# Attention and two MLP layers on one core: the first token block kept on chip, Pool's work cut into pieces of 128 columns, second banks for h and y

## The chip, the cores and the metric

The kernel runs on one core of a Trainium2 chip. The metric is device time in microseconds (us), the median of several executions. Engines are named as in the profile: PE (matrix products), DVE (vector engine), ACT (scalar engine), POOL (GpSimd), SP (issues DMAs).

## The reference

```python
# q, k, v: (4, 8, 576, 64); x: (2304, 512); float32 values, 2304 = 4 * 576
scores = scale * q @ k.T
thresh = max(scores, -1) - tau                       # tau = 0.02
scores = where(scores >= thresh, scores, -1e9)
attn = exp(scores - max(scores, -1))
attn = attn / (sum(attn, -1) + 1e-9)
x = (attn @ v).transpose(0, 2, 1, 3).reshape(2304, 512)
h = x @ w_in                                         # 512 x 2048
x = (h / (1 + exp(-h))) @ w_out                      # 2048 x 512
x = ((x @ w_a) * (x @ w_b)) @ w_out2                 # 512 x 1536, 1536 x 512
```

The weights arrive as 64-bit floating point; the kernel sees each number as two 32-bit words.

## The kernel before

**Stages.** Attention is cut into 144 softmax tiles of 128 query rows by 576 keys. `softmax` makes one: `scores` (PE), `lowest` (DVE: negated scores and their minimum), `threshold` (DVE, one column, L497), `exp` (ACT), `mask` (DVE, L506, with the row sums as a by-product). The first 16 tiles are "early": they alternate between two PSUM banks (`sa`, `sb`) and read the scores from PSUM; the later ones read a copy in SBUF. `weigh` collects the tiles of half a head pair (4 tiles for 256 query rows, 5 for 320): PE turns the masked tiles, multiplies with v into bank `av`, ACT copies the result out (`evacuate`). The inverse row sums are turned by PE too, stored to DRAM (`r_d`), loaded back spread over 64 partitions each (`xi`), Pool multiplies (`divide`, L618), and x goes to DRAM (`xT_d`).

MLP1 runs over 9 blocks of 256 tokens and 16 slices f of the hidden size, 144 units. `load_x` loads a block of x (four quarters, `xr`) and splits it into a high part (ACT) and the rest (Pool, `xl`, L676). A unit is `mlp1_up`, 12 products of 256 columns into bank `hb` (L699), tanh on ACT, `gate` on DVE (L711, reads `hb` and releases it), a split of g on ACT and DVE (L717), and `mlp1_down`, 12 products (L746) that add up in `sb` over the 16 units of a block. After a block, ACT and DVE empty `sb` (L765). Up of unit n stands ahead of down of unit n-1. There is one `hb` and one `sb`; the early tiles use `sb` for scores as well.

MLP2 has 60 units (blocks of 512 tokens, 12 slices): 12 products into `ps_a`, 12 into `ps_b` (L825), ACT copies `ps_a`, DVE multiplies by `ps_b` (`z`, L835), the split into `zh` (ACT) and `zl` (DVE, L841), then 12 products into the outputs `op` (L869).

**Weights.** They pass `split_weight` in chunks of 128 x 512: 32 for MLP1, all of which a block of MLP1 needs, and 36 for MLP2, where the first four have room of their own and the others wait until block 8 of MLP1 has let go of MLP1's weights. The steps of a chunk: DMA into `wraw`, `low` (ACT), `scale` (ACT for MLP1, L317; DVE for MLP2, L319), `sign` (DVE, L323), `join` (DVE, L328), `total` (POOL, the sum of the two words, L332), `hi` (ACT, L336), `lo` (L340: Pool for MLP1, alternately Pool and DVE for MLP2). The scaled half `wc` has one buffer, which `total` releases; `wraw` and `wt` have two.

**Order.** No engine's order is written by hand. A planner (`Plan`) holds every step as a task with an engine, a cost, a rank, the tasks it needs, and rings of buffers it takes and releases. `run` plays through time: an engine that is idle takes the ready task with the lowest rank, and that order is emitted. So a cost or a ring that is altered can move instructions on every engine. Attention's ranks are the tile numbers (0 to 143), the weights of MLP1 spread from 2 in steps of 1.3, MLP1 lies from 1000, MLP2 from 1e5, and MLP2's weights from 1e6: PE takes work of MLP1 only where attention has none ready.

The planner has a rule for DVE and Pool, which it takes to share a way to memory:

```python
if t["port"]:
    shared = max(0, min(port["Pool" if e == "DVE" else "DVE"] - now, t["cost"]))
    port[e] = end = done = end + self.SHARED * shared
```

A task lengthens by the time for which the other engine's current one still runs.

## Time and profile before

| | |
|---|---|
| median of three runs | 1202.97 us (1200.87 to 1204.55) |
| the profiled execution | 1202.49 us, its span 1200.7 us |
| busy: PE, DVE, ACT, POOL | 97%, 54%, 45%, 23% |
| moved by DMA | 90.14 MB |
| chain that ended last | PE 76%, DVE 10%, DMA 5%, issue 4%, ACT 4%, POOL 1% |

All views are of one execution. A line number (L506) is one of the kernel above; "z<-ps_b,z" is what is written and what is read, by the program's names; "128x512" is partitions by elements. In a group, "x36 | 36.4, 1011 | 5.3 <-ACT e L503 5.0" reads: 36 instructions, 36.4 us in all, 1011 ns each; the engine was idle for 5.3 us just ahead of them, 5.0 of it ended by ACT's line 503. In a timeline the first number is the start in us, the second the duration, and the bracket the idle time ahead with what ended it. PEclk is the clock granted to PE, 1.00 being 2.4 GHz.

### The profile page before, as it was taken

To read this page: it belongs to the slowest core of one execution; us is meant where nothing else is said; L and a number is where in the kernel's file an instruction comes from. 1 tells how busy PE (TensorE), PEld (TensorE's weight loads), DVE (VectorE), ACT (ScalarE), POOL (GpSimd) and SP (SyncE) were. 2 spreads that over 40 slices of the span, in tenths; PEclk is the share of its full clock that TensorE was granted. 3 is DMA by queue.
4 is the path that set the end of the run, shared out by engine and by line. 5 is a ranking of instruction groups with operands and counts; after the bars stand their busy time and mean duration, and the time that the engine had idled before them with its cause. 6 is when DMAs were issued, how large, how long until landed. Compare 5 with 4: busy or idle time off the path is not lost.

```text
span 1200.7 us, 19670 instructions
## 1 busy us (share of the span) xinstructions
PE 1162.6 (97%) x7675; PEld 998.2 (83%) x7675; DVE 648.1 (54%) x1428; ACT 544.5 (45%) x1071; POOL 278.9 (23%) x232
## 2 busy tenths in 40 slices
PE   8889989999999999989999999999999999999998
PEld 5556667888888888889999999888888888888898
DVE  7989898777777777473233258765311211221121
...
GB/s 190 195 176 150 160 152 129 80 85 86 97 72 71 89 89 32 101 166 36 1 37 27 1 66 117 152 123 71 70 1 1 70 1 1 18 36 1 1 36 18
DMA packets 43276, 90.14 MB, mean 75 GB/s; under 512 B 4384, under 2 KB 22448, under 8 KB 43184
## 3 DMA queue, kind: packets, MB, share of 16 engines
...
q10 hardware_dynamic: 144, 0.00, 0.0%
...
## 4 chain that ended last, share of the span: by engine, by line
PE 76%; DVE 10%; DMA 5%; issue 4%; ACT 4%; POOL 1%; SPq 0%; DVEq 0%; ACTq 0%; POOLq 0%
PE op L869 12%; PE ps_b L825 12%; PE ps_a L825 12%; PE hb L699 12%; PE sb L746 12%; PE av L583 5%; PE tp L538 5%; PE sa L473 4%; DVE e L506 3%; DMA xi<-r_d 2%; DVE t L489 1%; DVE wraw L323 1%; DVE thr L497 1%; DVE wc L328 1%; DVE gl L717 1%
## 5 line engine op out<-in xcount | busy, mean ns | idle before, releaser
L699 PE MATMUL hb<-xh,w 128*128 128x256 f32 x1152 | 225.1, 290 | 6.0 <-DVE th L711 3.9
L699 PEld LDWEIGHTS hb<-xh,w 128*128 128x128 f32 x1152 | 179.3, 192 | 14.2 <-DVE th L711 6.2
L746 PE MATMUL sb<-gh,w 128*128 128x256 f32 x1152 | 169.6, 286 | 2.3 <-DVE yo L765 1.8
L699 PE MATMUL hb<-xl,w 128*128 128x256 f32 x576 | 162.9, 283 | 0.0
L835 DVE TENSOR_TENSOR z<-ps_b,z 128x512 f32<-128x512 f32 (+1 forms) x60 | 38.2, 636 | 230.2 <-PE ps_b L825 230.2
L746 PEld LDWEIGHTS sb<-gh,w 128*128 128x128 f32 x1152 | 150.5, 192 | 6.6 <-DVE yo L765 2.8
L506 DVE SCALAR_TENSOR_TENSOR e<-t,thr,e 128x576 f32<-128x576 f32 x128 | 129.7, 1014 | 21.8 <-ACT e L503 20.8
L825 PE MATMUL ps_a<-yh,w 128*128 128x512 f32 (+1 forms) x480 | 137.0, 370 | 0.0
L825 PE MATMUL ps_b<-yh,w 128*128 128x512 f32 (+1 forms) x480 | 136.6, 369 | 0.0
L869 PE MATMUL op<-w,zh 128*128 128x512 f32 x432 | 134.3, 392 | 0.0
L489 DVE TENSOR_SCALAR_CACHE_REDUCE t<-sa,nscale 128x576 f32<-128x576 f32 x128 | 103.6, 809 | 51.6 <-PE sa L473 49.6
L538 PE MATMUL tp<-ident,e 128*128 128x128 f32 x706 | 106.5, 280 | 13.9 <-DVE e L506 10.0
L711 DVE SCALAR_TENSOR_TENSOR th<-th,hb 128x256 f32<-128x256 f32 x144 | 60.2, 418 | 107.2 <-ACT th L708 106.8
L332 POOL TENSOR_TENSOR wt<-wc,wt 128x512 uint32<-128x512 uint32 x68 | 91.2, 1342 | 109.5 <-DVE wc L328 91.3
L503 ACT ACTIVATE e<-t,min 128x576 f32<-128x576 f32 x128 | 99.6, 780 | 28.2 <-DVE t L489 27.5
L708 ACT ACTIVATE th<-hb 128x256 f32<-128x256 f32 x144 | 55.0, 382 | 122.3 <-PE hb L699 113.2
L699 PEld LDWEIGHTS hb<-xl,w 128*128 128x128 f32 x576 | 110.1, 191 | 0.0
L538 PEld LDWEIGHTS tp<-ident,e 128*128 128x128 f32 x706 | 78.8, 141 | 37.4 <-DVE e L506 16.7
L832 ACT COPY z<-ps_a 128x512 f32<-128x512 f32 (+1 forms) x60 | 32.5, 542 | 162.5 <-PE ps_a L825 162.4
L825 PEld LDWEIGHTS ps_a<-yh,w 128*128 128x128 f32 x480 | 87.5, 188 | 16.7
L825 PEld LDWEIGHTS ps_b<-yh,w 128*128 128x128 f32 x480 | 86.8, 188 | 15.4
L717 DVE TENSOR_TENSOR gl<-th,gh 128x256 fp32r<-128x256 f32 x144 | 76.0, 528 | 36.8 <-ACT gh L714 36.4
...
## 6 DMA issues: line engine op xcount, KB each, us to landing
...
```

The source lines that it names most:

```text
L332: nc.gpsimd.tensor_tensor(out=s["t"], in0=s["c"].bitcast(U32), in1=s["t"], op=ALU.add)
L489: nc.vector.tensor_scalar(out=s["t"], in0=s["s"][:, :, :NH], scalar1=nscale, scalar2=None, op0=ALU.mult, op1=ALU.min, accum_out=s["min"])
L503: nc.scalar.activation(out=s["e"], in_=s["t"], func=AF.Exp, scale=-1.0, bias=s["min"])
L506: nc.vector.scalar_tensor_tensor(out=s["e"], in0=s["s"][:, :, :NH] if early else s["t"], scalar=s["thr"], in1=s["e"], op0=ALU.is_ge if ear ...
L538: nc.tensor.transpose(t["tp"][:, j * P:(j + 1) * P], e["e"][:, o:o + P], ident)
L583: nc.tensor.matmul(s["av"][h * D:(h + 1) * D, :nq], lhsT=v["v"][:, h, k], rhs=s["p"][:, k, h * nq:(h + 1) * nq], start=(k == 0), stop=(k = ...
L699: nc.tensor.matmul(s["h"], lhsT=w[:, a, o:o + P], rhs=xx, start=(c == 0 and k == 0), stop=(c == NC - 1 and k == 2))
L711: nc.vector.scalar_tensor_tensor(out=s["t"], in0=s["t"], scalar=1.0, in1=s["h"], op0=ALU.add, op1=ALU.mult)
L717: nc.vector.tensor_sub(out=s["gl"], in0=s["t"], in1=s["gh"].bitcast(F32))
L746: nc.tensor.matmul(ys[j][:, e, :], lhsT=w[:, a, e * P:(e + 1) * P], rhs=gs[j, f][g], start=(f == 0 and e % 2 == 0 and a == 1), stop=(f == ...
L825: nc.tensor.matmul(s[nm][:, :tn], lhsT=w[:, a, o:o + P], rhs=yy[:, :tn], start=(c == 0 and k == 0), stop=(c == NC - 1 and k == 2))
L869: nc.tensor.matmul(o_ps[t0, i], lhsT=s[z][:, i * P:(i + 1) * P], rhs=wt["o2", f][:, a, :], start=(f == 0 and k == 0), stop=(f == NF2 - 1 a ...
```

## The change

1. *x of block 0.* The first 256 query rows of the first batch are block 0 of MLP1. For them (`stays`) the inverse sums are written 64 times side by side by a wide reciprocal, four small products by the identity spread them over the partitions of bank `av`, ACT copies x and the inverses in one piece of 512 columns, Pool divides, and `split_x` (what `load_x` did inline) splits from there. The 16 DMAs of these four weighings go.
2. *Pieces.* Pool's `total`, `lo` of weights and of q, `divide` and `xl` are issued as instructions of 128 columns (107 to 115 where the size doesn't divide). The planner's rule for the port changes: DVE now waits only to the end of the current piece. Pool's planned cost gets 90 ns for each piece.
3. *Columns.* `guard` and `threshold` take their added constant from a column of SBUF.
4. *k's low part* (20 head splits from tile 54 on) moves from Pool to DVE.
5. *Second banks.* From unit 64 on, odd units of MLP1 use bank `hc` instead of `hb`; from block 4 on, even blocks use `sd` instead of `sb`. Both live in a pool that opens when attention has closed. The two banks of MLP2's `ps_a` and `ps_b` become two pools: one opens with attention's end, the other after MLP1.

```diff
+TWO_H = 64
+PIECE = 128
...
-                        shared = max(0, min(port["Pool" if e == "DVE" else "DVE"] - now, t["cost"]))
-                        port[e] = end = done = end + self.SHARED * shared
+                        other, piece = port["Pool" if e == "DVE" else "DVE"]
+                        end = done = end + (max(0, other - now) % piece if e == "DVE" else max(0, other - now))
+                        port[e] = end, pool_ns(PIECE)
...
 def pool_ns(n):
-    return int(2.35 * n + 90)
+    return int(2.35 * n + 90 * len(pieces(n)))
+
+def pieces(n):
+    k = -(-n // PIECE)
+    return [slice(n * i // k, n * (i + 1) // k) for i in range(k)]
...
         def total():
-            nc.gpsimd.tensor_tensor(out=s["t"], in0=s["c"].bitcast(U32), in1=s["t"], op=ALU.add)
+            for o in pieces(512):
+                nc.gpsimd.tensor_tensor(out=s["t"][:, o], in0=s["c"][:, o].bitcast(U32), in1=s["t"][:, o], op=ALU.add)
...
-            eng = nc.gpsimd if lo_engine == "Pool" else nc.vector
+            eng, parts = (nc.gpsimd, pieces(512)) if lo_engine == "Pool" else (nc.vector, [slice(0, 512)])
...
         def lo_k():
-            nc.gpsimd.tensor_tensor(...)
+            nc.vector.tensor_tensor(...)
...
-        q, k = (add("Pool", pool_ns(S), n + R_SPLIT, f, [up]) for f in (lo_q, lo_k))
+        q = add("Pool", pool_ns(S), n + R_SPLIT, lo_q, [up])
+        k = add("DVE", dve_ns(S), n + R_SPLIT, lo_k, [up], port=True)
...
         def guard():
-            ... scalar1=EPS, scalar2=None, op0=ALU.add)
+            ... scalar1=eps, scalar2=None, op0=ALU.add)
...
+            if wide:
+                s["wide"] = x_p.tile([P, 320], F32, name="xi")[:, :m * D].rearrange("p (m d) -> p m d", d=D)
+                nc.vector.reciprocal(out=s["wide"], in_=s["sum"][:, :m].rearrange("p (m o) -> p m o", o=1).broadcast_to((P, m, D)))
...
-                nc.vector.tensor_add(out=s["thr"], in0=s["min"], in1=tadd)
+                nc.vector.tensor_scalar(out=s["thr"], in0=s["min"], scalar1=tadd, scalar2=None, op0=ALU.add)
...
+        stays = b == 0 and half == 0
...
+            if stays:
+                for k in range(4):
+                    nc.tensor.matmul(s["av"][k // 2 * D:(k // 2 + 1) * D, nq + k % 2 * P:][:, :P], lhsT=inv["wide"][:, k, :], rhs=ident,
+                                     start=True, stop=True, skip_group_check=True)
...
+        if stays:
+            dv = add("Pool", pool_ns(nq), last_n + R_EV, divide, [ev])
+            att_tasks.append(split_x(0, c, lambda: s["x"], [dv], "x")[1])
+            return es
...
+        bank = "hc" if n >= TWO_H and n % 2 else "hb"
...
+        ring = "sd" if j * NF >= TWO_H and j % 2 == 0 else "sb"
...
-        pools["ab"] = pool(ctx, "ps_ab", 2, "right", space=PSUM)
+        pools["hc"] = pool(p1, "ps_hc", 1, space=PSUM)
+        pools["ab", 0] = pool(ctx, "ps_ab", 1, "right", space=PSUM)
...
+        pools["ab", 1] = pool(ctx, "ps_ab2", 1, space=PSUM)
```

Costs, rings and the port rule together give a new order. Ahead of tile 52 there are 14 units of MLP1 on PE now, where there were 16. Three places:

POOL, in the first chunks of weights (`L332`/`L344` is the sum, `L340`/`L353` the low part, `L618`/`L649` the division of x by its sums, `L676`/`L705` the rest of x; "x4" is four instructions in a row). Before:

```order
L332 TENSOR_TENSOR wt<-wc,wt 128x512
L340 TENSOR_TENSOR w<-wt,w 128x512
L332 TENSOR_TENSOR wt<-wc,wt 128x512
L618 TENSOR_TENSOR x<-x,xi 128x256
L340 TENSOR_TENSOR w<-wt,w 128x512
L332 TENSOR_TENSOR wt<-wc,wt 128x512
L340 TENSOR_TENSOR w<-wt,w 128x512
L676 TENSOR_TENSOR xl<-xr,xh 128x256
```

And now:

```order
L649 TENSOR_TENSOR x<-x 128x128 x2
L344 TENSOR_TENSOR wt<-wc,wt 128x128 x4
L705 TENSOR_TENSOR xl<-x,xh 128x128 x2
L353 TENSOR_TENSOR w<-wt,w 128x128 x4
L344 TENSOR_TENSOR wt<-wc,wt 128x128 x4
L353 TENSOR_TENSOR w<-wt,w 128x128 x4
L344 TENSOR_TENSOR wt<-wc,wt 128x128 x4
L649 TENSOR_TENSOR x<-x 128x128 x2
L353 TENSOR_TENSOR w<-wt,w 128x128 x4
```

Each sum and each low part is four instructions; x is divided and split between them without a load ahead of it.

DVE, in MLP2, from the product of unit 7 on (`L319`/`L330` scale, `L323`/`L334` sign, `L328`/`L339` join, `L340`/`L353` the low part of every second chunk). Before:

```order
L835 TENSOR_TENSOR z<-ps_b,z 128x512
L841 TENSOR_TENSOR zl<-z,zh 128x512
L319 TENSOR_SCALAR wc<-wraw 128x512
L340 TENSOR_TENSOR w<-wt,w 128x512
L323 TENSOR_SCALAR wraw<-wraw 128x512
L328 SCALAR_TENSOR_TENSOR wc<-wc,wraw 128x512
L319 TENSOR_SCALAR wc<-wraw 128x512
L323 TENSOR_SCALAR wraw<-wraw 128x512
L328 SCALAR_TENSOR_TENSOR wc<-wc,wraw 128x512
L835 TENSOR_TENSOR z<-ps_b,z 128x512
```

And now:

```order
L883 TENSOR_TENSOR z<-ps_b,z 128x512
L889 TENSOR_TENSOR zl<-z,zh 128x512
L330 TENSOR_SCALAR wc<-wraw 128x512
L353 TENSOR_TENSOR w<-wt,w 128x512
L334 TENSOR_SCALAR wraw<-wraw 128x512
L339 SCALAR_TENSOR_TENSOR wc<-wc,wraw 128x512
L330 TENSOR_SCALAR wc<-wraw 128x512
L334 TENSOR_SCALAR wraw<-wraw 128x512
L339 SCALAR_TENSOR_TENSOR wc<-wc,wraw 128x512
L330 TENSOR_SCALAR wc<-wraw 128x512
L334 TENSOR_SCALAR wraw<-wraw 128x512
L353 TENSOR_TENSOR w<-wt,w 128x512
```

Three chunks begin where two did between one product and the next: DVE is given MLP2's weights in a closer order.

PE, in MLP2 at unit 8 (`L825`/`L873` are the products into `ps_a` and `ps_b`, `L869`/`L917` the ones into the outputs; the last chunk of this unit is the 32nd of MLP2's). Before:

```order
L825 MATMUL ps_a<-yl,w 128x512
L825 MATMUL ps_a<-yh,w 128x512 x2
L825 MATMUL ps_a<-yl,w 128x512
L825 MATMUL ps_b<-yh,w 128x512 x2
L825 MATMUL ps_b<-yl,w 128x512
L825 MATMUL ps_b<-yh,w 128x512 x2
L825 MATMUL ps_b<-yl,w 128x512
L825 MATMUL ps_b<-yh,w 128x512 x2
L825 MATMUL ps_b<-yl,w 128x512
L825 MATMUL ps_b<-yh,w 128x512 x2
L825 MATMUL ps_b<-yl,w 128x512
L869 MATMUL op_9786<-w,zh 128x512 x2
```

And now:

```order
L873 MATMUL ps_a<-yl,w 128x512
L917 MATMUL op_10199<-w,zh 128x512 x2
L917 MATMUL op_10199<-w,zl 128x512
L917 MATMUL op_10204<-w,zh 128x512 x2
L917 MATMUL op_10204<-w,zl 128x512
L917 MATMUL op_10211<-w,zh 128x512 x2
L917 MATMUL op_10211<-w,zl 128x512
L917 MATMUL op_10221<-w,zh 128x512 x2
L917 MATMUL op_10221<-w,zl 128x512
L873 MATMUL ps_a<-yh,w 128x512 x2
L873 MATMUL ps_a<-yl,w 128x512
L873 MATMUL ps_b<-yh,w 128x512 x2
```

The twelve products of unit 7 into the outputs, which followed all of unit 8's, now stand between those into `ps_a`, and `ps_b` comes after them. Between the seventh and the 32nd chunk of MLP2 lie 25 chunks, in the old order and in the new.

## Rows read from the trace of the kernel before

**Rows 1.** The page, part 1: busy us, share of the span, instructions.

```profile
PE 1162.6 (97%) x7675; PEld 998.2 (83%) x7675; DVE 648.1 (54%) x1428; ACT 544.5 (45%) x1071; POOL 278.9 (23%) x232
```

**Rows 2.** Busy time by stretch; columns: stretch, each engine's busy us, PEclk, DMA, GB/s.

```profile
0.00:57.00 57.00, 47.32 (x323) 31.30 (x323) 48.14 (x122) 44.33 (x78) 27.60 (x29) 1.00 0.59 194
57.00:190.00 133.00, 121.27 (x860) 86.90 (x860) 122.29 (x265) 101.24 (x202) 77.14 (x60) 0.97 0.49 153
190.00:490.00 300.00, 293.57 (x2350) 259.75 (x2350) 225.32 (x594) 197.52 (x379) 88.41 (x72) 1.00 0.25 82
490.00:545.00 55.00, 50.42 (x397) 48.41 (x394) 32.81 (x62) 23.54 (x54) 15.00 (x13) 0.97 0.44 141
...
705.00:752.00 47.00, 45.24 (x353) 43.17 (x352) 36.28 (x64) 24.98 (x52) 21.72 (x16) 1.00 0.36 113
```

**Rows 3.** Groups of instructions by form, 57 to 190 us, DVE and PE.

```profile
L506 DVE SCALAR_TENSOR_TENSOR e<-t,thr,e 128x576 f32<-128x576 f32 x36 | 36.4, 1011 | 5.3 <-ACT e L503 5.0
...
L323 DVE TENSOR_SCALAR wraw<-wraw 128x512 uint32<-128x512 uint32 x23 | 20.9, 909 | 3.0 <-ACT wc L317 3.0
...
L497 DVE TENSOR_TENSOR thr<-min,tadd 128x1 f32<-128x1 f32 x35 | 13.6, 390 | 0.3
...
L699 PE MATMUL hb<-xh,w 128*128 128x256 f32 x124 | 26.5, 305 | 1.5 <-POOL w L340 1.5
```

**Rows 4.** Groups by form, whole span: the mask of an early tile.

```profile
L506 DVE SCALAR_TENSOR_TENSOR e<-sa,thr,e 128x576 f32<-128x576 f32 x8 | 6.5, 814 | 1.2 <-ACT e L501 1.2
```

**Rows 5.** Timeline of POOL, then of DVE, MLP2's weights (start us, us, instruction).

```profile
765.84 1.29 POOL L332 TENSOR_TENSOR wt<-wc,wt 128x512 uint32<-128x512 uint32 x1 [1.10 <-DVE wc L328]
...
769.40 1.30 POOL L332 TENSOR_TENSOR wt<-wc,wt 128x512 uint32<-128x512 uint32 x1 [2.27 <-DVE wc L328]
...
771.42 1.35 POOL L340 TENSOR_TENSOR w<-wt,w 128x512 fp32r<-128x512 f32 x1 [0.73 <-ACT w L336]
...
773.41 1.67 POOL L332 TENSOR_TENSOR wt<-wc,wt 128x512 uint32<-128x512 uint32 x1 [0.63 <-DVE wc L328]
...
767.62 0.43 DVE L323 TENSOR_SCALAR wraw<-wraw 128x512 uint32<-128x512 uint32 x1
...
771.65 1.68 DVE L328 SCALAR_TENSOR_TENSOR wc<-wc,wraw 128x512 uint32<-128x512 uint32 x1
```

**Rows 6.** Timeline of PE around attention's end.

```profile
499.68 0.40 PE L699 MATMUL hb<-xh,w 128*128 128x256 f32 x2
...
502.56 0.40 PE L699 MATMUL hb<-xh,w 128*128 128x256 f32 x2
...
507.05 0.50 PE L699 MATMUL hb<-xh,w 128*128 128x256 f32 x2 [1.46 <-DVE th L711]
...
513.39 1.96 PE L746 MATMUL sb<-gh,w 128*128 128x256 f32 x8 [1.76 <-DVE yo L765]
...
526.40 0.50 PE L699 MATMUL hb<-xh,w 128*128 128x256 f32 x2 [1.18 <-DVE th L711]
```

**Rows 7.** Timeline of POOL at 29 and 50 us, then of DVE at 50 us.

```profile
29.35 0.73 POOL L618 TENSOR_TENSOR x<-x,xi 128x256 f32<-128x256 f32 x1 [1.09 <-DMA xi<-r_d]
...
50.13 1.29 POOL L340 TENSOR_TENSOR w<-wt,w 128x512 fp32r<-128x512 f32 x1 [0.96 <-ACT w L336]
...
51.38 0.92 POOL L676 TENSOR_TENSOR xl<-xr,xh 128x256 fp32r<-128x256 f32 x1
...
50.72 0.08 DVE L506 DVE_READ_ACCUMULATOR e<-sb,thr,e 128x1 f32 x1
```

**Rows 8.** Timeline of PE, first and last of ten units of MLP1's last stretch.

```profile
715.81 0.40 PE L699 MATMUL hb<-xh,w 128*128 128x256 f32 x2
...
744.37 0.41 PE L699 MATMUL hb<-xh,w 128*128 128x256 f32 x2
```

**Rows 9.** Timeline of DVE, then of PE: the 32nd chunk of MLP2's weights.

```profile
816.01 0.69 DVE L340 TENSOR_TENSOR w<-wt,w 128x512 fp32r<-128x512 f32 x1
...
817.58 0.62 PE L825 MATMUL ps_b<-yh,w 128*128 128x512 f32 x2
```

More of the change, by code (lines that the diff above doesn't have):

```diff
@@ L125, in run @@
         pipe, window, cold, spans = 0, 0, False, [(0, 4400)]
-        port = {"DVE": 0, "Pool": 0}
+        port = {"DVE": (0, 1), "Pool": (0, 1)}
         free = 0
@@ L448, in finish @@
             gd = add("DVE", 150, n + R_NORM, guard, masked)
-            return add("DVE", 150, n + R_NORM, inverse, [gd], ["rs"])
-        return total, finish
+            return add("DVE", dve_ns(m * D) if wide else 150, n + R_NORM, inverse, [gd], ["xi" if wide else "rs"])
+        return total, finish, s
     counter = [0]
@@ L602, in evacuate @@
         def evacuate():
-            s["x"] = x_p.tile([P, 320 + P], F32, name="x")
-            nc.scalar.copy(out=s["x"][:, :nq + P], in_=s["av"][:, :nq + P])
+            s["x"] = x_p.tile([P, 512], F32, name="x")
+            m = 2 * nq if stays else nq + P
+            nc.scalar.copy(out=s["x"][:, :m], in_=s["av"][:, :m])
         def store_sums():
@@ L617, in divide @@
         def divide():
-            nc.gpsimd.tensor_tensor(out=s["x"][:, :nq], in0=s["x"][:, :nq], in1=s["i"][:, :nq], op=ALU.mult)
+            for o in pieces(nq):
+                nc.gpsimd.tensor_tensor(out=s["x"][:, o], in0=s["x"][:, o], in1=s["x"][:, nq:][:, o] if stays else s["i"][:, o], op=ALU.mult)
         def store():
@@ L657, in fused_kernel, with split_x, hi, lo @@
     up_last, down_last, y_dma = [None], [None], []
+    def split_x(j, c, src, after, ring):
+        s = xs.setdefault(j, {})
+        def hi():
+            s["h", c] = xb_p.tile([P, TB], F32R, name="xh")
+            s["l", c] = xb_p.tile([P, TB], F32R, name="xl")
+            nc.scalar.copy(out=s["h", c], in_=src()[:, :TB])
+        def lo():
+            for o in pieces(TB):
+                nc.gpsimd.tensor_tensor(out=s["l", c][:, o], in0=src()[:, o], in1=s["h", c][:, o].bitcast(F32), op=ALU.subtract)
+        h = pl.add("ACT", act_ns(TB), R_AUX, hi, after, ["xb"])
+        l = pl.add("Pool", pool_ns(TB), R_AUX, lo, [h])
+        pl.free(ring, l)
+        x_ready[j, c] = (h, l)
+        return h, l
     def load_x(j):
-        s = xs[j] = {}
+        s = xs.setdefault(j, {})
         def split(c):
@@ L693, in fn @@
                 if c == 0:
-                    s["h"] = ps_1.tile([P, 512], F32, name="hb")[:, :TB]
+                    s["h"] = (pools["hc"] if bank == "hc" else ps_1).tile([P, 512], F32, name=bank)[:, :TB]
                 w = wt["in", c, f // 4]
@@ L721, in mlp1_up @@
             p = pl.add("PE", 3 * pe_ns(TB), R, up(c),
-                       [*x_ready[j, c], *w_ready["in", c, f // 4]], ["hb"] if c == 0 else [], behind=[up_last[0]])
+                       [*x_ready[j, c], *w_ready["in", c, f // 4]], [bank] if c == 0 else [],
+                       behind=[up_last[0], *([closed] if c == 0 and bank == "hc" else [])])
             up_last[0] = p
@@ L728, in mlp1_up @@
         ga = pl.add("DVE", dve_ns(TB), R_AUX, gate, [th])
-        pl.free("hb", ga)
+        pl.free(bank, ga)
         hh = pl.add("ACT", act_ns(TB), R_AUX, hi, [ga])
@@ L753, in mlp1_down @@
             p = pl.add("PE", 4 * pe_ns(TB), R, down(k0), [g_ready[j, f][k0 == 8], *w_ready["out", f]],
-                       ["sb"] if f == 0 and k0 == 0 else [], behind=[down_last[0]])
+                       [ring] if f == 0 and k0 == 0 else [], behind=[down_last[0]])
             down_last[0] = p
@@ L846, in mlp2_up @@
                 p = pl.add("PE", 3 * pe_ns(tn), 1e5 + 2 * n, up(nm, c), [*y2_ready[t0, c], *w_ready[nm, c, f // 4]],
-                           ["z" + nm] if c == 0 else [], behind=[up_last[0]])
+                           ["z" + nm] if c == 0 else [], behind=[up_last[0], *([closed1] if n % 2 and c == 0 else [])])
                 up_last[0] = p
@@ L907, in fused_kernel, with close_attention @@
             pair(b, c, (0, 1))
+    def close_attention():
+        att.close()
+        right.close()
+        open_transit()
+        pools["w2"] = pool(ctx, "wpool2", RINGS["w2"], "right")
+        pools["y"] = pool(ctx, "yb", 6, "right")
+        pools["hc"] = pool(p1, "ps_hc", 1, space=PSUM)
+        pools["ab", 0] = pool(ctx, "ps_ab", 1, "right", space=PSUM)
+    closed = pl.add("none", 1, 0, close_attention, behind=[*att_tasks, *closed0])
     units = [(j, f) for j in range(NB) for f in range(NF)]
     for n, u in enumerate(units):
-        if u[1] == 0:
+        if u[1] == 0 and u[0]:
             load_x(u[0])
```

59 lines of the change are left out of this document (24 added, 35 removed).

## The prediction, as recorded before the result

> **What bounds the kernel now.** I read the page first: PE is busy 97% of the span [rows 1]. So the time is PE's work plus the places where PE stands, and a gain can only come from those. Dividing the span at the stage borders [rows 2] shows where they are: PE stands for 9.7 of the first 57 us, for 11.7 of the next 133, for 6.4 of the 300 in which attention and MLP1 share PE, for 4.6 in the 55 us around attention's end, and for 1.8 in MLP1's last 47; the granted clock is 1.00, but 0.97 in two of them. MLP2 has hardly any such place. The reader is to see that in each stretch something else holds PE. In the first 190 us it is DVE, busy 48.1 of 57 and 122.3 of 133 us, and part of that busy time is waiting. Row by row from 57 to 190 [rows 3]: the mask takes 1011 ns, while the same instruction with its scores in PSUM takes 814 [rows 4]; the sign step takes 909, against 0.43 us in a calm moment (767.62 in [rows 5]); the threshold of a single column takes 390. At attention's end it is the one h bank and the one y bank: PE waits 1.46 and 1.18 us for the gate that reads h, and 1.76 us for y's evacuation [rows 6].
>
> **The port.** Why DVE is slow is seen where the two engines' rows are laid side by side [rows 7]. DVE's sign step starts at 50.72, in the middle of a 512-column Pool instruction (50.13, 1.29 long), and ends at 51.71, which is 0.29 after that one's end. The next Pool instruction starts back to back at 51.38 and takes 0.92, where its like at 29.35 takes 0.73. So a DVE instruction of this kind waits for the end of Pool's, is let in before the next one, and Pool then waits for it. Pieces shorten DVE's wait and lengthen Pool's work.
>
> **The change, part by part.**
>
> *A piece of 128 columns.* The trace has none; 512 columns take 1.30 [rows 5] and 256 take 0.73 [rows 7], so 2.23 ns a column and 0.16 us fixed, of which 0.04 overlaps the next instruction (50.13 + 1.29 = 51.42 against 51.38). Four pieces then take 4 x 0.445 - 3 x 0.04 = 1.66 us, 0.36 more than one, before DVE steps in between. The Trainium skill would have the fixed part smaller: its GPSIMD Engine Reference, Elementwise — side-by-side cycle accounting, gives 4497 ns for 2048 columns at 2.6 cycles each, which leaves 60 ns. By that estimate four pieces cost 0.18 more, a chunk of MLP2 some 0.2, and the forecast below would be 1194. No row of this kernel has so short a fixed part, so the rows' 0.16 stands.
>
> *Weights and attention, 0 to 190 us.* From 57 to 190, 23 chunks pass the sign's count in [rows 3], one in 5.78 us. With pieces Pool needs for one of them 1.66 (the sum), 0.72 (the copy between: 769.40 + 1.30 to 771.42 in [rows 5]), 1.66 (the low part), some 0.5 for x, and what DVE slips in: 36 masks of 0.81 and 23 signs of 0.43 make 1.7 us per chunk, and Pool is at work for some 3.8 of 5.8, so 1.1. That is 5.64: Pool takes over where DVE held the pace. DVE gets back 36 x 0.2 + 23 x 0.48 = 18 us and what the threshold waits, but spends it waiting for Pool's next result. 0.14 x 23 is 3 us faster; against it the new order leaves 14 instead of 16 units of MLP1 in front of tile 52, to be done later. I take **-2 us**; a doubt of 0.4 us per chunk either way makes the ends **-9 and +9**.
>
> *x of block 0 on chip.* Sixteen DMAs go, and x is there after a copy and four Pool pieces. By itself it is worth nothing: block 0 of MLP1 needs all 32 chunks, and these come one in 5.78 us. PE's up products already wait for Pool's weights here (1.5 us, [rows 3]). The sixteen small products, the four wider copies and the four wider reciprocals lie in the 57 us in which PE stands for 9.7: nothing either.
>
> *Threshold and guard with a column operand* are in the relief above. *k's low part on DVE:* twenty of 576 columns, at most 0.81 each [rows 4], 16 us in a stretch in which DVE is busy 225 of 300 [rows 2], and Pool loses as much. With DVE's slack as its cover it costs nothing; without that, up to 16 us. For 190 to 490, where PE stands 6.4 us, I take **-2** for shorter waits (ends -5 and +1).
>
> *Second banks.* From 502.56 to 526.40 PE begins six units [rows 6], 23.84 us; an undisturbed one takes 2.88 (499.68 to 502.56), so 6.6 were lost, the half clock included. The wait at 507.05 is that of unit 64 for the gate of 63; both still use the first bank, so its 1.6 stay. 5 are saved, and 1 at later block borders: **-6** (ends -7 and -3). In MLP1's last stretch nine units take 28.56 us [rows 8] instead of 25.9: 2.6 more could be saved.
>
> *The weights of MLP2.* Here it is given back. These chunks start when block 8 of MLP1 lets go of its first weight, and unit 8 of MLP2 needs the 32nd of them: its last low part starts at 816.01 and ends at 816.70, and PE takes it at 817.58 [rows 9]. The slack is 0.9 us. The chain runs scale, sign and join on DVE, sum on Pool, and only then the next scale: 3.56 us where the low part is DVE's (765.84 to 769.40), 4.01 where it is Pool's (769.40 to 773.41), because the join (771.65, 1.68 long) waits for it and ends 0.56 after it [rows 5]. With pieces the first is 3.56 + 0.36 = 3.92. The second is 1.66 + 0.72 + 0.41 (first piece) + 0.56 (the join's turn) + 1.25 (the other three) = 4.60, because Pool must finish them before the next sum. That is 0.48 more per chunk, and by the order 25 chunks lie between the seventh and the 32nd: 11.9, and 0.7 for the first two steps. PE's new order puts 12 products of unit 7 (2.75 us) ahead of that wait, which costs nothing and covers as much. 11.9 + 0.7 - 0.9 - 2.75 = 9 us later than before, whatever PE saved since block 8 began, so the 2.6 are lost as well. The sign and zl also wait less in pieces, which no row prices: I take **+7.5** (ends -2.6, which is no wait at all, and +11).
>
> *Sum:* -2 - 2 - 6 + 7.5 = -2.5 us. The profiled execution took 1202.49 (span 1200.7), 0.5 under the median of 1202.97, so **1200** is forecast, with 1196 to 1205 as this case's own range. A measurement of this kernel can tell 0.3%, 3.6 us, from no change: the band is 1199.4 to 1206.6.
>
> **The rivals.**
> 1. *The chain of weights keeps pace*, and the gains stay: -2 - 2 - 6 - 2.6 = -12.6, 1190. For it: DVE's steps wait less, and in the old order a wait was avoided by 0.9 us only, so the planner steers close. Against: the sum of rows above. It decides at 0.15 us more per chunk (0.9 + 2.75 over 25).
> 2. *Slower: Pool's port in the first 190 us.* If DVE slips in more often than I count, a chunk takes 6.1 instead of 5.78 us: 23 x 0.35 = 8 us on attention's way, since ACT's scale and DVE's join queue behind Pool's sum, with exp and mask behind them. Instead of -2 that makes 1200 + 2 + 8 = 1210. For it: Pool is busy 77 of 133 us, gets 46 x 0.36 = 17 more, and shares the rest. It decides from 5.78 up.
> 3. *DVE's relief passes through* to attention: 9 us less there instead of 2, 1193. For it: DVE is busy 92% of that stretch. Against: the scaled half of a weight has one buffer, so DVE cannot run ahead of Pool.
> 4. *Pieces don't let DVE in*, so the change doesn't do what it says: waits last up to 1.66 instead of 1.30, a quarter more of 25 us, and the chain is as above: 1209. Against: [rows 7].
>
> **How the numbers follow.** The forecast gets 0.42, the rivals 0.20, 0.20, 0.12 and 0.06. Faster by over 0.3%: rivals 1 and 3, and 0.12 for the part of the forecast's range that lies under 1199.4, 0.44. Within 0.3%: the rest of it and the near end of rival 2, 0.33. Slower: 0.23. The range takes in rivals 1 to 4 but for their far ends: 1189 to 1211.
>
> **What would show it.** Right: PE stands 5 us or more before the last chunk of MLP2's unit 8; the pieces of a sum start some 0.41 apart; no wait for y or h after unit 65; the mask comes to 850 ns or so in the first 190 us, while chunks still pass one in 5.6 to 5.9 us. Wrong: MLP2 without a wait (rival 1); chunks over 6 us apart before 190 (rival 2), or under 5.3 (rival 3); DVE waiting over 0.5 us within Pool's four pieces (rival 4).

## The result, and the profile after

| | before | changed |
|---|---|---|
| the profiled execution | 1202.49 us, span 1200.7 | 1215.29 us, span 1213.5 |
| ratio, 95% interval | 1 | 1.0113 [1.0077, 1.0149] |
| forecast | | 1200 (1189 to 1211) |

The change made the kernel slower by some 13 us, outside the range. Two of its four executions, of 1406.91 and 3260.01 us, were slow ones and stand in no comparison; the other two took 1215.29 and 1218.29 us. The page's first part and the same stretches as before, with two more in MLP2 (columns as in [rows 2]):

```profile
PE 1172.4 (97%) x7699; PEld 1002.7 (83%) x7699; DVE 614.3 (51%) x1449; ACT 543.7 (45%) x1071; POOL 374.0 (31%) x730
```

```profile
0.00:57.00 57.00, 45.82 (x317) 31.09 (x317) 45.87 (x115) 42.33 (x73) 36.53 (x84) 1.00 0.51 166
57.00:190.00 133.00, 121.06 (x850) 86.14 (x852) 106.41 (x265) 99.55 (x197) 108.90 (x205) 0.97 0.50 153
190.00:490.00 300.00, 297.08 (x2386) 262.90 (x2385) 221.49 (x618) 200.26 (x389) 107.14 (x193) 1.00 0.26 82
490.00:545.00 55.00, 50.71 (x402) 49.66 (x402) 31.54 (x64) 23.79 (x55) 22.07 (x43) 0.97 0.45 141
...
705.00:752.00 47.00, 45.41 (x348) 43.10 (x348) 29.92 (x61) 23.59 (x50) 30.84 (x60) 1.00 0.36 112
752.00:805.00 53.00, 53.00 (x230) 42.88 (x229) 30.17 (x53) 21.62 (x36) 31.75 (x70) 1.00 0.38 118
805.00:840.00 35.00, 29.66 (x107) 21.81 (x105) 19.82 (x35) 13.45 (x22) 21.29 (x46) 0.85 0.33 108
```

PE gained nothing where DVE was relieved: from 57 to 190 us DVE is busy 106.4 instead of 122.3 us, and PE 121.06 instead of 121.27. The time went in MLP2: from 805 to 840 PE stands for 5.3 of 35 us, and its granted clock is 0.85, a mix of both levels. In the kernel before that stretch is full:

```profile
805.00:840.00 35.00, 35.00 (x154) 28.57 (x153) 21.39 (x33) 13.35 (x22) 13.32 (x11) 1.00 0.23 76
```

The timeline of PE there, in the changed kernel:

```profile
811.12 0.62 PE L917 MATMUL op<-w,zh 128*128 128x512 f32 x2
...
814.50 0.73 PE L873 MATMUL ps_a<-yh,w 128*128 128x512 f32 x2 [1.14 <-POOL w L353]
...
817.39 1.22 PE L917 MATMUL op<-w,zh 128*128 128x512 f32 x2 [1.93 <-ACT zh L886]
...
820.26 1.05 PE L917 MATMUL op<-w,zh 128*128 128x512 f32 x2
...
823.47 0.73 PE L873 MATMUL ps_a<-yh,w 128*128 128x512 f32 x2 [0.46 <-POOL w L353]
...
828.37 0.73 PE L873 MATMUL ps_b<-yh,w 128*128 128x512 f32 x2 [1.82 <-DVE w L353]
```

Three of the four waits are for weights. The fourth, for zh, comes from them too, by way of ACT: in ACT's order the first step of a chunk, which waits for POOL's low part, stands ahead of that zh:

```profile
816.17 0.66 ACT L323 ACTIVATE wt<-wraw 128x512 uint32<-128x512 uint32 x1 [2.31 <-POOL w L353]
816.74 0.60 ACT L886 CAST zh<-z 128x512 fp32r<-128x512 f32 x1
```

Behind the first two waits, two products take 1.05 us together instead of 0.62: the lower clock, after PE had stood. It was granted twice, in these stretches:

```profile
816.20:823.00 6.80, 5.61 (x12) 3.64 (x12) 3.68 (x7) 3.08 (x5) 3.37 (x9) 0.50 0.43 148
829.90:833.30 3.40, 3.40 (x10) 2.63 (x9) 2.61 (x5) 1.24 (x2) 2.67 (x6) 0.50 0.45 154
```

The weights' pace is seen on POOL:

```profile
766.29 1.71 POOL L344 TENSOR_TENSOR wt<-wc,wt 128x128 uint32<-128x128 uint32 x4 [2.70 <-ACT z L880]
768.73 2.22 POOL L353 TENSOR_TENSOR w<-wt,w 128x128 fp32r<-128x128 f32 x4 [0.73 <-ACT w L348]
770.91 1.71 POOL L344 TENSOR_TENSOR wt<-wc,wt 128x128 uint32<-128x128 uint32 x4
775.32 0.88 POOL L344 TENSOR_TENSOR wt<-wc,wt 128x128 uint32<-128x128 uint32 x2 [2.70 <-ACT z L880]
```

A sum of four pieces takes 1.71 us where one of 512 columns took 1.29 [rows 5], and the sums start 4.62 and 4.41 apart. In the middle of the low part (2.22 instead of 1.71) DVE's join came in, the first row here: the piece that started at 769.20 took 0.91, the three others 0.45 to 0.51. So had the prediction read [rows 7], with the second row, the sign step of the kernel before:

```profile
768.96 0.83 DVE L339 SCALAR_TENSOR_TENSOR wc<-wc,wraw 128x512 uint32<-128x512 uint32 x1
...
50.72 0.99 DVE L323 TENSOR_SCALAR wraw<-wraw 128x512 uint32<-128x512 uint32 x1
```

At attention's end the waits of [rows 6] for y and for the second gate are gone, but a longer one is new. ACT, then PE:

```profile
503.62 0.67 ACT L323 ACTIVATE wt<-wraw 128x512 uint32<-128x512 uint32 x1 [2.29 <-DMA wraw<-w_a]
504.19 0.37 ACT L753 ACTIVATE th<-hb 128x256 f32<-128x256 f32 x1
```

```profile
505.76 0.80 PE L744 MATMUL hb<-xh,w 128*128 128x256 f32 x2 [3.08 <-DVE th L756]
```

ACT's order has the first step of MLP2's first chunk ahead of a tanh of MLP1. That step waits 2.29 us for its DMA, the tanh stands behind it, and PE waits 3.08 us for the gate behind the tanh. (On DVE the same chunk's first three steps, from 503.69 on, stand ahead of that gate as well.) The products that wait are those of unit 63; the second banks come into use behind it.

### The profile page after: what moved, and what is told of

It reads as the page before. It is cut to its first block, busy times and chain, and to the rows that moved or that the text cites. A ratio compares the mean times of both kernels' runs of the same rounds, so it can differ in the third digit from the quotient of the medians.

```text
span 1213.5 us, 20314 instructions
## 1 busy us (share of the span) xinstructions
PE 1172.4 (97%) x7699; PEld 1002.7 (83%) x7699; DVE 614.3 (51%) x1449; ACT 543.7 (45%) x1071; POOL 374.0 (31%) x730
## 5 line engine op out<-in xcount | busy, mean ns | idle before, releaser
L744 PE MATMUL hb<-xh,w 128*128 128x256 f32 x832 | 164.3, 292 | 5.4 <-DVE th L756 4.7
L344 POOL TENSOR_TENSOR wt<-wc,wt 128x128 uint32<-128x128 uint32 x272 | 127.4, 499 | 76.7 <-DVE wc L339 55.6
L873 PE MATMUL ps_a<-yh,w 128*128 128x512 f32 (+1 forms) x480 | 139.4, 375 | 1.6 <-POOL w L353 1.6
L873 PE MATMUL ps_b<-yh,w 128*128 128x512 f32 (+1 forms) x480 | 138.1, 372 | 1.8 <-DVE w L353 1.8
L744 PEld LDWEIGHTS hb<-xh,w 128*128 128x128 f32 x832 | 129.9, 192 | 11.9 <-DVE th L756 6.1
L353 POOL TENSOR_TENSOR w<-wt,w 128x128 fp32r<-128x128 f32 x200 | 112.2, 590 | 84.5 <-ACT w L348 84.5
L917 PE MATMUL op<-w,zh 128*128 128x512 f32 x432 | 136.4, 397 | 1.9 <-ACT zh L886 1.9
L744 PE MATMUL hb<-xl,w 128*128 128x256 f32 x416 | 118.0, 284 | 0.0
L794 PE MATMUL sb<-gh,w 128*128 128x256 f32 x768 | 116.7, 287 | 0.0
L561 PEld LDWEIGHTS tp<-ident,e 128*128 128x128 f32 x706 | 79.2, 141 | 35.1 <-issue 12.8
L873 PEld LDWEIGHTS ps_a<-yh,w 128*128 128x128 f32 x480 | 88.0, 189 | 20.2 <-POOL w L353 2.7
L794 PEld LDWEIGHTS sb<-gh,w 128*128 128x128 f32 x768 | 101.3, 191 | 3.2 <-issue 2.0
L873 PEld LDWEIGHTS ps_b<-yh,w 128*128 128x128 f32 x480 | 86.6, 188 | 19.5 <-DVE w L353 2.3
L917 PEld LDWEIGHTS op<-w,zh 128*128 128x128 f32 x432 | 81.2, 190 | 19.7 <-ACT zh L886 2.4
L886 ACT CAST zh<-z 128x512 fp32r<-128x512 f32 (+1 forms) x60 | 34.5, 575 | 125.6 <-DVE z L883 125.6
L873 PE MATMUL ps_a<-yl,w 128*128 128x512 f32 (+1 forms) x240 | 89.7, 374 | 0.0
```

Source lines behind the costliest of these rows:

```text
L344: nc.gpsimd.tensor_tensor(out=s["t"][:, o], in0=s["c"][:, o].bitcast(U32), in1=s["t"][:, o], op=ALU.add)
L353: eng.tensor_tensor(out=wt[key][:, 1, o], in0=s["t"][:, o].bitcast(F32), in1=wt[key][:, 0, o].bitcast(F32), op=ALU.subtract)
L561: nc.tensor.transpose(t["tp"][:, j * P:(j + 1) * P], e["e"][:, o:o + P], ident)
L744: nc.tensor.matmul(s["h"], lhsT=w[:, a, o:o + P], rhs=xx, start=(c == 0 and k == 0), stop=(c == NC - 1 and k == 2))
L794: nc.tensor.matmul(ys[j][:, e, :], lhsT=w[:, a, e * P:(e + 1) * P], rhs=gs[j, f][g], start=(f == 0 and e % 2 == 0 and a == 1), stop=(f == ...
L873: nc.tensor.matmul(s[nm][:, :tn], lhsT=w[:, a, o:o + P], rhs=yy[:, :tn], start=(c == 0 and k == 0), stop=(c == NC - 1 and k == 2))
```

## The experiments

For all runs one table, worked out from each trace. "Chunk" is the distance of ACT's copies (`hi`), from the 8th to the 32nd of MLP1's weights and from the seventh to the 31st of MLP2's, divided by 24. "Rest" is the span after the end of attention's last mask, brought to 57 finished units of MLP1 by 2.88 us a unit; it leaves out attention, whose last mask ended between 481.2 and 488.7 in ten executions with the same order up to there; totals of single executions carry that spread. "MLP2" is from MLP1's last gate to the end, "unit" a steady unit of MLP2 (products z of the 18th and 48th, by 30). For 11, 12, 14 and 17 "us" is the median of several executions, and the other columns are of one of them (in 14 one of 1199.93 us); elsewhere all are of one execution.

| kernel | us | chunk, MLP1 | chunk, MLP2 | rest | MLP2 | unit |
|---|---|---|---|---|---|---|
| before | 1202.49 | 5.74 | 4.16 | 716.4 | 452.0 | 8.267 |
| changed | 1215.29 | 6.13 | 4.67 | 731.1 | 467.2 | 8.351 |
| 1 MLP2's chunks whole | 1208.03 | 6.15 | 4.37 | 722.4 | 459.4 | 8.351 |
| 2 no shift | 1216.33 | 6.15 | 4.67 | 727.7 | 464.2 | 8.267 |
| 3 before, shift | 1206.45 | 5.80 | 4.18 | 719.3 | 455.8 | 8.351 |
| 4 before, banks | 1204.46 | 5.73 | 4.15 | 716.4 | 451.9 | 8.267 |
| 5 all whole, same order | 1208.96 | 6.13 | 4.34 | 719.0 | 458.7 | 8.351 |
| 6 one bank | 1216.13 | 6.12 | 4.66 | 730.5 | 465.7 | 8.351 |
| 7 x by DRAM | 1213.74 | 6.20 | 4.67 | 727.3 | 465.8 | 8.351 |
| 8 no pieces, new order | 1206.42 | 5.73 | 4.29 | 719.5 | 458.8 | 8.351 |
| 9 before, MLP2 in pieces | 1216.95 | 5.76 | 4.61 | 728.8 | 461.2 | 8.267 |
| 10 second wc | 1218.15 | 6.13 | 3.88 | 730.5 | 461.9 | 8.351 |
| 11 all mended | 1217.44 | 6.17 | 5.00 | 730.0 | 473.7 | 8.267 |
| 12 mended, whole | 1214.29 | 5.65 | 4.73 | 726.7 | 469.3 | 8.267 |
| 13 early loads, MLP2 whole | 1199.65 | 6.15 | 4.26 | 711.9 | 456.6 | 8.267 |
| 14 the same, second wc | 1195.59 | 6.16 | 3.93 | 709.4 | 452.7 | 8.267 |
| 15 before, early loads | 1202.96 | 5.77 | 4.14 | 713.4 | 451.9 | 8.267 |
| 16 no pieces, early loads | 1200.45 | 5.73 | 4.26 | 713.2 | 454.9 | 8.267 |
| 17 as 14, one bank | 1204.33 | 6.13 | 4.04 | 716.2 | 452.5 | 8.267 |

Timed with intervals were 11 (1.0115 [1.0091, 1.0139]), 12 (1.0099 [1.0074, 1.0123]), 14 (0.993 [0.9905, 0.9954]) and 17 (1.0003 [0.9986, 1.002]); the others are one execution, beside which the kernel before took 1205.77 (1 to 4), 1203.85 (5 to 8), 1203.61 (9 and 10, a median of seven) and 1203.22 (13, 15, 16). The theory at first: the loss is MLP2's chain of weights, lengthened by the pieces. Its rival: the new order.

**1. MLP2's chunks whole.** The emission alone, so that the order stays:

```diff
-            for o in pieces(512):
+            for o in pieces(512) if key[0] in ("in", "out") else [slice(0, 512)]:
```

> The changed kernel with Pool's sum and low part of MLP2's 36 chunks as one instruction of 512 columns each; the order on every engine stays that of the changed kernel. Theory (the four pieces lengthen each chunk, and PE waits for the 32nd of them and loses clock behind the wait): a chunk comes every 4.1 to 4.2 us between the seventh and the 31st instead of 4.67, PE no longer stands 5.3 us before unit 8, the granted clock is 1.00 from 805 to 840 us, and the time falls by about 10 us, from 1215 to 1205. Rival (the new order on DVE makes the chunks slow, not the pieces): 4.5 us or more a chunk, PE still waits, 1212 or more.

4.37 lies between theory and rival, and so does the time: in this order pieces account for 0.30 of the 0.51 us a chunk, and the order for the rest. PE waits 1.6 us in place of 5.3, at full clock:

```profile
752.00:805.00 53.00, 53.00 (x230) 42.87 (x230) 37.10 (x59) 23.71 (x39) 25.30 (x20) 1.00 0.44 128
805.00:840.00 35.00, 33.45 (x144) 26.46 (x143) 24.52 (x38) 14.76 (x24) 15.66 (x13) 1.00 0.33 104
```

**9. The pieces alone, in the old order.** The kernel before with the same two loops for MLP2's chunks and nothing else (every other engine's order unchanged).

> The kernel before, in its own order, with Pool's sum and low part of MLP2's chunks in four pieces of 128 columns, and nothing else. Theory (the prediction's term, 0.36 us more on each sum and, where the low part is Pool's, the wait for it: 0.48 a chunk): 4.16 us a chunk becomes 4.6 to 4.7 between the seventh and the 31st, PE waits some 10 us ahead of the end of unit 8's products into ps_b, and loses clock behind it; 1202.5 becomes 1212 to 1217. Rival (as in the changed kernel's order, where the pieces were worth 0.30 a chunk): 4.4 to 4.5 a chunk, 1207 to 1211.

4.61 us a chunk, as the theory has it, and a loss as large as that of the whole change: 13 us, 12.4 of it after attention and 9.2 of that in MLP2. The stretches of [rows 2]'s view, where PE stood for 3.1 and 2.8 us:

```profile
752.00:805.00 53.00, 49.91 (x227) 40.49 (x226) 30.79 (x55) 22.45 (x38) 33.33 (x69) 1.00 0.42 125
805.00:840.00 35.00, 32.21 (x135) 24.54 (x134) 19.48 (x35) 13.16 (x22) 22.42 (x48) 1.00 0.40 121
```

The granted clock did not fall here, as the theory had it do. The waits lie spread from 754 to 849 us, those of the changed kernel between 813 and 828. MLP1's last block took 2.6 us longer as well (50.9 instead of 48.3, from its first gate to its last).

**2, 3, 4. Why is a steady unit of MLP2 slower?** No part of the prediction had this. Either the weights' place in SBUF (the changed kernel has one column of constants more, which moves the weights that lie above it by 32 bytes; y and the first four chunks of MLP2 lie elsewhere and stay) or the banks of `ps_a` and `ps_b`.

```diff
 # 2, changed kernel
-    eps = const.tile([P, 1], F32, name="eps")
-    back = const.tile([P, 1], F32, name="back")
+    both = const.tile([P, 2], F32, name="both")
+    eps, back = both[:, :1], both[:, 1:]
 # 3, kernel before
+    const.tile([P, 1], F32, name="unused")
 # 4, kernel before
...
-        pools["ab"] = pool(ctx, "ps_ab", 2, "right", space=PSUM)
+        pools["ab", 0] = pool(ctx, "ps_ab", 1, "right", space=PSUM)
+        pools["ab", 1] = pool(ctx, "ps_ab2", 1, "right", space=PSUM)
```

> The changed kernel with eps in one tile of SBUF with another constant, so that all of the weights lie at the addresses they had before (in the changed kernel they lie 32 bytes higher). Theory (the shift of the weights against y makes the products into ps_a and ps_b slower): a steady unit of MLP2 takes 8.24 to 8.28 us again instead of 8.33 to 8.36, and the time falls by 5 us to 1210. Rival (the banks in which ps_a and ps_b lie make the difference): a unit stays at 8.33 to 8.36, 1215.

> The kernel before with one unused column of constants more, which moves the weights up by 32 bytes and changes nothing else. Theory (the shift): a steady unit of MLP2 takes 8.33 to 8.36 us, and the time rises by 5 us to 1207 or 1208. Rival (the banks): 8.24 to 8.28 as before, 1202 to 1204.

> The kernel before with ps_a and ps_b of MLP2 in two pools, so that a unit uses banks 4 and 5 and the next 6 and 7, as in the changed kernel (before: 4 or 5 and 6 or 7). Theory (the shift of the weights): 8.24 to 8.28 us a unit as before, 1202 to 1204. Rival (the banks): 8.33 to 8.36, 1207 or 1208.

The shift it is, both ways. Products z of the 18th and the 48th unit on DVE, in run 3, then in run 2:

```profile
894.53 0.69 DVE L836 TENSOR_TENSOR z<-ps_b,z 128x512 f32<-128x512 f32 x1 [6.29 <-PE ps_b L826]
...
1145.04 0.69 DVE L836 TENSOR_TENSOR z<-ps_b,z 128x512 f32<-128x512 f32 x1 [0.77 <-PE ps_b L826]
```

```profile
906.78 0.69 DVE L883 TENSOR_TENSOR z<-ps_b,z 128x512 f32<-128x512 f32 x1 [6.21 <-PE ps_b L873]
...
1154.79 0.69 DVE L883 TENSOR_TENSOR z<-ps_b,z 128x512 f32<-128x512 f32 x1 [0.74 <-PE ps_b L873]
```

Thirty units take 250.51 us with the shift and 248.01 without it. All of MLP2 is 3.8 us longer in run 3 than in the kernel before. The total of run 2 didn't fall with it, since attention ended 4.5 us later there; MLP2 itself is 3.0 shorter (464.2).

**5 and 8. Pieces in the first 190 us.** In 5 all of Pool's operations are issued whole in the changed order; in 8 the planner knows of it (`PIECE = 576`; the second y bank also waits for attention's end explicitly there, as in 12 and 16).

> The changed kernel with every one of Pool's operations issued whole, in the changed kernel's order. Theory (the pieces pace the chunks of MLP1's weights): from the eighth to the 32nd of these a chunk takes 5.7 to 5.8 us instead of 6.1, while the mask from 57 to 190 us goes back from under 900 ns to about 1000; the end of attention moves by under 3 us either way, MLP2's chunks are as in the run with those alone whole, and the time is 1206 to 1210. Rival (the new order paces the chunks): 6.0 us or more a chunk with whole operations too, and attention's last mask over 3 us later, since DVE's waits are back: 1211 or more.

> The change without its pieces: the size of a piece is 576 columns, so that Pool's operations are whole in the planner and in the program, and the order follows from that; the second y bank waits for attention's end explicitly. Theory (the pieces are what costs time): 5.7 to 5.8 us a chunk of MLP1's weights, 4.1 to 4.2 of MLP2's, no wait of PE at unit 8 of MLP2, 1203 to 1207, which still holds the 4 to 5 us that the shifted weights cost. Rival (DVE's relief by pieces is worth more in attention than it costs): attention's last mask comes 5 us or more later, 1211 or more.

With whole operations a chunk of MLP1's weights still takes 6.13 us in the changed order, and 5.73 in the order that the planner makes for whole ones: the order sets this pace, not Pool. The theory falls here, and its rival holds for the pace, but not for the time, which stays under its 1211. Groups of run 5, then of the changed kernel, from 57 to 190 us:

```profile
L529 DVE SCALAR_TENSOR_TENSOR e<-t,thr,e 128x576 f32<-128x576 f32 x35 | 35.8, 1024 | 4.9 <-ACT e L526 4.4
L338 DVE TENSOR_SCALAR wraw<-wraw 128x512 uint32<-128x512 uint32 x22 | 20.5, 931 | 2.8 <-ACT wc L332 2.7
L520 DVE TENSOR_SCALAR thr<-min,tadd 128x1 f32<-128x1 f32 x36 | 7.4, 206 | 0.4
```

```profile
L525 DVE SCALAR_TENSOR_TENSOR e<-t,thr,e 128x576 f32<-128x576 f32 x35 | 31.6, 904 | 7.8 <-ACT e L522 7.4
...
L334 DVE TENSOR_SCALAR wraw<-wraw 128x512 uint32<-128x512 uint32 x22 | 13.0, 589 | 13.9 <-ACT wc L328 13.9
L516 DVE TENSOR_SCALAR thr<-min,tadd 128x1 f32<-128x1 f32 x36 | 7.4, 206 | 0.4
```

The pieces do let DVE in: the mask 904 instead of 1024 ns, the sign step 589 instead of 931. Attention's last mask ends at 488.2 in run 5 and between 481.2 and 488.7 in the executions with pieces, so what DVE saves comes out as more idle time ahead of it (13.9 us before the sign step), and not as an earlier end that could be told from the spread. The threshold takes 206 in both: its gain over 390 [rows 3] comes from the operand's form, not from the pieces.

**6 and 7. One bank; x by DRAM.** `TWO_H = 1000`, and `stays = False`.

> The changed kernel without the second banks for h and y (the unit from which they are used set past the last one); up to attention's end its order is the same. Theory (they save PE's waits for y's evacuation and for one gate, and 1 us at later borders): 3 to 5 us slower, 1218 to 1221, with waits of over 1 us for y and for the gate after unit 64. Rival (the one wait that is left, for a gate behind ACT's weight step, sets this stretch whatever the banks are): within 1.5 us, 1214 to 1217.

> The changed kernel with x of block 0 sent through DRAM as before; all else, pieces and banks too, as changed. Theory (block 0 of MLP1 waits for weights, not for x): within 2 us, 1213 to 1218, and the first gate of MLP1 comes 5 to 10 us later without any effect on attention's end. Rival (x on chip is what keeps PE busy in the first 57 us): 3 us or more slower, 1219 or more.

Both change nothing that counts. In 7 that was foreseen. In 6 the second banks prove worth nothing as the changed kernel stands; run 17 tells why.

**10 to 12. Mending the chain.** 10 gives MLP2's chunks a second `wc`, so that a scale needn't wait for Pool's sum; 11 adds the place of eps and 4 us of planned landing time for all loads of y and of MLP2's weights; 12 is 11 with `PIECE = 576`.

```diff
 # 10 to 12
...
-            s["c"] = pools["wtmp"].tile([P, 512], F32, name="wc")
+            s["c"] = pools["wtmp"].tile([P, 512], F32, name="wc", bufs=RINGS[ring])
...
 # 11, 12
...
-        a = dma(rank, P * 4096, load, take=["wraw"], behind=after)
+        a = dma(rank, P * 4096, load, take=["wraw"], behind=after, slack=0 if key[0] in ("in", "out") else LATE)
```

> The changed kernel with a second buffer for the scaled half of MLP2's weights (wc), so that the scale of a chunk needn't wait for Pool's sum of the one before; the pieces stay, and the order follows from the planner. Theory (a chain through that one buffer paces MLP2's chunks, and the pieces lengthen it): 3.5 us a chunk or less, no wait at unit 8, no fall of the clock there, and 1215 becomes 1204 to 1207 with the shifted weights still in it. Rival (DVE, shared with Pool, is the pace itself): over 4.3 us a chunk, PE waits, 1211 or more.

> The changed kernel, pieces and banks and x on chip included, with three edits: eps in one tile with another constant (no shift of the weights), the second wc buffer, and 4 us more of planned landing time for the loads of y and of MLP2's weights, so that the planner doesn't put steps that wait for them ahead of MLP1's tanh on ACT. Theory (these three places are where the change lost its gain): no wait of over 1 us after attention's end, a steady unit of MLP2 at 8.24 to 8.28 us, 1195 to 1200, ratio to the kernel before 0.992 to 0.998. Rival (the change loses in attention's stage too): 1203 or more.

> The same three edits on the change without its pieces (Pool's operations whole, 576 columns a piece). Theory (with the chain in MLP2 broken, the pieces matter little there; in attention they are worth 4 us or less to DVE): 1193 to 1199, within 4 us of the run with pieces. Rival (whole operations cost attention over 5 us): slower than the run with pieces by 5 us or more.

All three totals missed. In 10 the buffer does break the chain (3.88 us a chunk, no wait for a weight), but the planner used it to put weight steps in front of MLP1's and MLP2's own, at attention's end PE stands 6.0 of 55 us (4.3 in the changed kernel), and its waits of 705 to 850 us are now these:

```profile
PE sd L795 <- ACT gh L760: 2.7, 5, 0.7
PE op L918 <- ACT zh L887: 2.0, 3, 0.9
PE op L918 <- DVE zl L890: 1.1, 1, 1.1
PE sd L795 <- DVE gl L763: 0.5, 1, 0.5
```

In 11 MLP1 ends at 740.8 instead of 746.3, for ACT's tanh no longer stands behind a load. But the landing time on every chunk stretched MLP2's chain to 5.00 (3.88 in 10, without it), and PE stands 17.2 us for it:

```profile
PE ps_a L875 <- POOL w L354: 17.2, 3, 7.8
```

**13 to 16. Landing time for the first loads alone.** Only the first four chunks and the first block of y get it; Pool is whole for MLP2's chunks, in the planner too; eps lies in the common tile. 14 has the second `wc` besides. 15 is the kernel before with the landing time alone, 16 the change without any piece.

```diff
+        a = dma(..., slack=LATE if 1e6 <= rank < 1e6 + 4 else 0)
+            ld = dma(..., take=["yr"], slack=LATE if t0 == 0 else 0)
```

> The changed kernel with eps in one tile with another constant, Pool whole for MLP2's chunks (in the planner and the program), and 4 us more of planned landing time for the first four chunks of MLP2's weights and the first loads of y alone. In the run with that time for all of these loads, attention's end lost its waits (MLP1 ended at 740.8 instead of 746.3), but MLP2's chunks came one in 5.0 us. Theory (the planner's landing times set ACT's order at attention's end, and, given to every chunk, spoil the order of MLP2's): MLP1 ends at 740 to 743, MLP2's chunks take 4.2 to 4.4 us, PE still waits a little at unit 8, 1198 to 1202. Rival (the 5.0 us came from the second wc buffer): chunks at 4.2 to 4.4 as well, but in the next run over 4.6.

> The same with the second wc buffer for MLP2's chunks. Theory (that buffer breaks the chain; in the run of the changed kernel with it alone a chunk took 3.88 us with pieces): 3.9 us a chunk or less, no wait of PE of over 0.5 us at units 6 to 8 of MLP2, MLP1's end at 740 to 744, 1192 to 1197. Rival (the buffer only moves DVE's work into MLP1's last stretch and MLP2's first units, as it did in that run, whose time didn't fall): small waits of 0.5 us each before the products of z, MLP1's end after 745, 1200 or more.

> The kernel before with nothing but those 4 us of planned landing time for the first four chunks of MLP2's weights and the first loads of y. Theory (the waits at attention's end come as much from ACT's order as from the single banks): the wait of 1.46 us for unit 63's gate goes, the one of 1.76 us for y stays or shrinks, MLP1 ends 2 to 4 us earlier, and MLP2's chunks, which start with MLP1's last block, stay at 4.16 us: 1199 to 1202. Rival (the single banks alone make them): MLP1 ends within 1 us of before, 1202 to 1205.

> The change without its pieces anywhere, with eps in one tile with another constant and the 4 us of landing time for the first four chunks and loads of y. Theory (pieces bring nothing that attention's end needs): MLP1 ends at 740 to 743 and MLP2's chunks take 4.2 to 4.3 us as in the run without pieces, 1197 to 1201, within 2 us of the run with pieces in attention alone. Rival (pieces shorten attention by the 4 us that they seemed to between 190 and 480 us): 3 us or more slower than that run.

13 came out as the theory has it: from attention's last mask to the last gate of MLP1's block 7 it takes 208.5 us, the changed kernel 214.0, and run 1, whose Pool is whole for MLP2 too, 214.1. So the landing time is worth some 5.5 us there. 14 came out nearly so (in its first execution, of 1192.75 us, MLP1 ended at 738.6, earlier than expected; a chunk took 3.93) and is faster than both kernels. 15 missed its theory: MLP1 ended no earlier (749.3), the wait for y went, and waits for gates stayed (3.1 us in three). Its part after attention is 3.0 us shorter all the same, which its total doesn't show, because its attention ended later. 16 lies within 1 us of 13: pieces in attention are worth nothing that can be told.

> The kernel that came out fastest (whole operations of Pool on MLP2's weights, no shift, planned landing time for the first four chunks and loads of y, second wc buffer), timed. Theory (its gain over the kernel before is real): 1191 to 1196, ratio 0.989 to 0.995, clear of 1. Rival (a fortunate execution): 1198 or more, ratio above 0.996.

1195.59, ratio 0.993 [0.9905, 0.9954].

**17. The second banks, once nothing else holds the stretch.** 14 with `TWO_H = 1000`.

> The same kernel without the second banks for h and y. Theory (the second banks are worth something only where no other wait holds the same stretch, which is so here): 3 to 6 us slower, MLP1's end at 742 to 745 instead of 738.6, waits of 1 us or more for gates and y's evacuation at attention's end and in MLP1's last 47 us, 1195 to 1199. Rival (they are worth nothing here either, as in the changed kernel, where leaving them out changed nothing): within 1.5 us.

Without them the gain is gone. The stretches around attention's end and at MLP1's last block, in the timed run of 14, then in 17:

```profile
490.00:545.00 55.00, 53.63 (x428) 50.56 (x427) 37.61 (x67) 24.76 (x58) 17.66 (x19) 1.00 0.46 141
...
705.00:752.00 47.00, 47.00 (x374) 46.04 (x373) 36.97 (x66) 26.57 (x56) 23.32 (x17) 1.00 0.40 118
```

```profile
490.00:545.00 55.00, 50.77 (x414) 49.76 (x414) 37.14 (x67) 24.14 (x55) 17.87 (x19) 1.00 0.46 141
...
705.00:752.00 47.00, 45.10 (x350) 43.15 (x350) 39.80 (x66) 26.98 (x56) 24.99 (x19) 1.00 0.42 128
```

and its waits of PE from 490 to 860 us are all for a gate that holds the one h bank:

```profile
PE hb L746 <- DVE th L758: 6.1, 9, 1.7
```

After attention 17 takes 716.2 us and 14 takes 709.4: the banks are worth 6.8, and 8.7 by the medians, more than the 3 to 6 of the theory. Up to the last gate of MLP1's block 7 they bring 3.1 us (210.2 from the last mask on, against 213.3), in the last block 3.8 (46.5 against 50.3).

## Why the prediction was wrong

Its terms against the changed kernel's profiled execution:

| stretch | forecast | measured |
|---|---|---|
| to attention's last mask, units evened out | -4 | -1.9 |
| from there to MLP1's last block (second banks) | -6 | +0.8 |
| MLP1's last block | 0 | -1.3 |
| MLP2 | +7.5 | +15.2 |
| sum | -2.5 | +12.8 |

- **MLP2's weights: right in mechanism, too small as a term (7.5 us forecast, 15.2 measured).** Four pieces were put at 1.66 us and take 1.71; a chunk was to take 0.48 more, and run 9, where the pieces are all that changed, has 0.45. That the changed kernel has 0.51 is partly luck: by run 1 the pieces make 0.30 of it, the new order the rest. The lower price that stood beside it, 0.18 more for four pieces by an estimate from the Trainium skill (GPSIMD Engine Reference, Elementwise — side-by-side cycle accounting), is not what the rows show: 1.71 - 1.29 is 0.42. PE stood 5.3 us, where 5 or more were named as the mark. What the step left out is the clock: 0.50 was granted for 10.2 us, of which 1.2 lie in a wait, so 4.5 us of work were lost; part of that lies in products that would have waited for weights anyway. And the 12 products of unit 7, counted as cover, had themselves to wait 1.93 us for zh, behind a weight step on ACT.
- **The second banks: -6 forecast, +0.8 measured; the step took the waits of [rows 6] as the banks' to remove.** In the new order ACT holds the same stretch with a step that waits for a DMA, at unit 63, where the banks are not in use yet, so that they bring nothing (run 6). With that step out of the way they bring 6.8 us (run 17). That this is near 6 is luck: 3.1 of it lie where the -6 stood, and 3.8 in MLP1's last block, where the prediction had seen 2.6 and counted them as lost. The order of ACT could be read beforehand; the prediction speaks of the orders of DVE, POOL and PE alone.
- **Weights and attention: the reason was wrong.** "Pool takes over where DVE held the pace" fails in run 5: the pace of 6.13 us is that of the new order, with pieces or without. Rival 2 named that pace (6.1) and gave the wrong cause for it; its 8 us did not come either, since by attention's end the two kernels are level within the spread (the -1.9 of the table too is less than that). DVE's relief is real and not on the way to the end.
- **x on chip at nothing: right** (run 7). Threshold and guard: right that they cost nothing, but the threshold's relief is the form's, and for the guard, of which only seven lie between 57 and 190 us, none can be told. k's low part was not tried by itself.
- **Not in the sum: the shift of the weights**, 3.8 of MLP2's 15.2 us (run 3). Counted from the start of one product to that of the next, PE lost 10.8 us in MLP2 at the waits and the lower clock: the 5.3 and 4.5 from above, and 1.0 at the edges of waits. Three products of MLP2 more than before were left when MLP1's last gate was done, 0.7 us. Together that makes 15.3.

What the prediction named as the marks held in part: PE had no wait for y or h after unit 65, and the pieces of a sum started 0.42 apart; the mask came to 904 ns, not 850, and chunks passed in over 6 us, the mark of rival 2.
